# Turnings of chunks 4 and 5 as whole 128x128 blocks, every step in another fixed order, and the weights loaded behind the first inputs

## The chip, the cores and the metric

The kernel runs on one core of one Trainium2 chip. The metric is the device time of one execution in microseconds (us), and lower is better. The engines are named as in the profile: PE (TensorE) with its weight loads PEld, DVE (VectorE), ACT (ScalarE), POOL (GpSimd) and SP (SyncE, which here only issues transfers).

## The reference

A recurrent attention layer is followed by a feed-forward block with squared ReLU. There are 4 batches, 8 heads, 768 time steps and a head size of 40; the inputs r, k, v, w, a and b have the shape [4, 8, 768, 40] in float32.

```python
for t in range(S):                       # S = 768, per batch b and head h
    y[:, :, t] = einsum('bhd,bhde->bhe', rt, state)
    Sa = einsum('bhde,bhe->bhd', state, at)
    state = state * wt[:, :, None, :] - einsum('bhd,bhe->bhde', Sa, bt) \
            + einsum('bhd,bhe->bhde', vt, kt)
x = y.transpose(0, 2, 1, 3).reshape(B * S, H * D)     # 3072 x 320
h = maximum(x @ w_in, 0)                              # w_in  320 x 2048
out = (h * h) @ w_out                                 # w_out 2048 x 320
```

## The kernel before

The 768 time steps are cut into 12 chunks of 64. The state is carried from chunk to chunk; inside a chunk the recurrence is written as matrix products with a triangular mask. All matrix work is in bf16 with sums in float32.

For each chunk c there are these steps; a step's name is its kind and its chunk, and a helper issues it, so the profile gives it the helper's line.

- Loads `ldw`, `lda`, `ldk`, `ldb`, `ldv`, `ldr`: SP issues two transfers of 160 KB for each, into buffers that exist twice. A load waits until the chunk two before has been read out of its buffer.
- Preparation. `ln`, `hi` and `lo` take the logarithm of w and split it into two bf16 parts; `cf` and `ce` sum it along time on PE, and `ef`, `ef i` and `eg` take exponentials on ACT (L595, L598, L528). `castK`, `castB`, `castA`, `castR` and `castV` turn inputs into bf16. In chunks 0 to 7 the casts are then turned on PE (transposed by a matrix product with the identity): `TK` (k and b), `TA`, `TR`, and later `BK` (the scaled k and b back), `TV` (v), `TS` (the state) and `XT` (the output). Their results are copied or multiplied out of PSUM by `tK`, `tA`, `tR`, `bK`, `tV`, `tS` and `xt`.
- Recurrence: `EN` and its mask `mEN` (L752), `AS` (needs the state of the chunk before), `EV`, `u0`, `NU`, `u1`, then the new state `SC`, `S` and `s`.
- Output of the recurrence: `CX` and `mCX`, `RS`, `Y`, `y`, `yd`, `XT`, `xt`.
- Feed-forward block in four parts u0 to u3: `F` (inner dimension 256) and `FL` (the last 64), `f` (ReLU), `q` (square), `O` (with w_out), then `o` and the store `st`. Chunk 11 splits `O` into `OA`, `OB` and `OC`.

A turning exists in two forms. The first turns the 64 upper and the 64 lower rows apart (`tp`, L409), with two small products side by side in the array. The second turns a whole 128x128 block in one product (`tpw`, L412), so that it has half as many products. The set `WHOLE` says for which chunks the second form is used.

The weights are loaded by POOL, which also converts them to bf16: `lwi 0 k0 x0` to `k1 x3` (eight pieces of w_in, one for each half of the inner dimension and each part u), `lwl 0` (the last 64 rows of w_in, two transfers) and `lwo 0 x0` to `x7` (w_out). Being instructions of POOL's queue, they wait for whatever POOL does ahead of them.

The order of everything is written out by hand, or rather as a long string `ORDER`: for every step it names the engine and, on PE, the PSUM slot 0 to 3 (`PE2 TK 4`). `WD2` entries are two products of ones whose result nobody reads; they fill PE's time at the start. Each engine runs its own steps strictly in that order, and a step waits for its inputs by semaphores. So the string sets three things: which engine does a step that could run on two or three, what stands in front of it there, and which PSUM slot it waits for.

The two forms, in the steps TK, and the loop that issues the string (a few lines of each):

```python
        if c in WHOLE:                                            # L622, in turned_first
            ms = [tpw(lambda i=i, y=y: slot(hb, BF16)[:, y].rearrange(...)[:, :, i, :],
                      lambda i=i, y=y: tKB[y][:, i].rearrange("p q e -> p (q e)"))
                  for i in range(8) for y in range(2)]
        pe(f"TK {c}", *tmode(c), ms, reads=[("tKB", 0), ("tKB", 1)], writes=[hb], alloc=[hb])

        for entry in text.replace("\n", " ").split(";"):          # L64, Plan.issue
            where, name = entry.split(None, 1)
            ...
            for h in o.alloc:
                self.slot_of[h] = int(where[len(eng):])
```

Of the kernel before, what the change touches and what calls it, by code (L numbers as in the profile page):

```python
# [87 lines left out]
0; SP ldb 0; POOL zr 0; DVE lo 0; SP ldv 0; POOL castA 0; PE1 ce 0; POOL zv 2; PE2 cf 0; POOL zr
1; SP lda 1; PE3 WD2; ACT ef 0; PE0 TA 0; SP ldw 2; DVE castB 0; ACT ln 1; DVE castK 0; ACT ef 0
i; PE3 TK 0; POOL hi 1; DVE tA 0 g0; SP ldk 1; DVE zv 0; POOL lo 1; ACT eg 0; DVE tA 0 g1; PE2  # L90
WD2; DVE tK 0 g1; SP ldb 1; ACT castA 1; POOL castV 0 g1; POOL castV 0 g0; PE2 cf 1; DVE tK 0 g0;
SP ldr 0; PE0 TA 1; ACT ef 1 i; PE1 EN 0 g1; SP ldr 1; PE3 WD2; DVE mEN 0 g1; ACT ln 2; PE3 EN 0
g0; SP ldk 2; ACT ef 1; POOL castK 1; DVE mEN 0 g0; PE1 WD2; PE1 WD2; ACT castB 1; SP ldb 2; DVE
tA 1 g1; PE1 ce 1; PE2 EV 0; POOL hi 2; DVE zv 1; PE3 TK 1; ACT u0 0 w; DVE tA 1 g0; SP ldv 1;
POOL lo 2; ACT u0 0 s1; DVE u0 0 s0; DVE tK 1 g0; PE NU 0; PE0 WD2; ACT u1 0 x0s0; PE0 BK 0; SP
ldb 3; DVE tK 1 g1; ACT u1 0 x0s1; ACT u1 0 x1s0; DVE bK 0; SP ldw 3; ACT u1 0 x1s1; PE3 EN 1 g1;
DVE mEN 1 g1; ACT castR 1; PE0 EN 1 g0; PE2 S 0 g0; PE S 0 g1; ACT eg 1; DVE s 0; POOL castV 1 g0;
PE3 TV 0; ACT castV 1 g1; DVE mEN 1 g0; POOL zk 1; PE1 AS 1; POOL castR 0; ACT tV 0; DVE zk 2;
POOL castK 2; PE EV 1; SP ldr 2; PE2 TR 0; DVE u0 1 s0; PE0 TR 1; ACT tR 0 g0; DVE tR 0 g1; SP lda
3; ACT tR 1 g0; DVE tR 1 g1; PE3 CX 0 g0; PE2 TS 0; ACT ln 3; DVE castB 2; PE0 WD2; SP ldv 2; DVE  # L100
tS 0; ACT u0 1 s1; PE0 cf 2; ACT u0 1 w; DVE mCX 0 g0; PE2 CX 0 g1; ACT ef 2 i; PE NU 1; SP lda 2;
DVE mCX 0 g1; PE3 TK 2; ACT u1 1 x0s0; ACT ef 2; SP ldv 3; DVE u1 1 x0s1; PE2 Y 0; ACT u1 1 x1s0;
PE0 BK 1; DVE yd 0; DVE y 0; ACT u1 1 x1s1; DVE tK 2 g0; ACT bK 1; PE2 ce 2; PE1 TV 1; POOL hi 3;
SP ldk 3; DVE tK 2 g1; ACT castV 2 g1; POOL lo 3; PE0 SC 1; ACT eg 2; DVE tV 1; SP ldw 4; PE3 XT
0; POOL lwi 0 k0 x2; PE S 1 g0; ACT xt 0; PE S 1 g1; POOL castA 2; PE2 cf 3; DVE s 1; PE1 CX 1 g0;
POOL lwi 0 k1 x2; PE3 CX 1 g1; DVE mCX 1 g0; ACT ef 3; PE0 TA 2; ACT ef 3 i; DVE mCX 1 g1; PE1 BK
2; PE2 RS 1; DVE tA 2 g1; POOL castK 3; ACT castB 3; PE Y 1; DVE tA 2 g0; ACT castV 2 g0; POOL
castR 2; PE3 TS 1; DVE yd 1; ACT bK 2; POOL lwl 0; DVE y 1; PE0 EN 2 g0; DVE mEN 2 g0; PE2 XT 1;
POOL lwi 0 k0 x1; ACT xt 1; POOL lwi 0 k1 x1; DVE za 0; PE1 F 0 u2; ACT tS 1; POOL castA 3; PE0 F
1 u2; POOL lwi 0 k0 x0; POOL lwi 0 k1 x0; PE2 EN 2 g1; POOL lwo 0 x2; PE3 TK 3; DVE mEN 2 g1; POOL  # L110
lwi 0 k1 x3; POOL lwi 0 k0 x3; PE FL 0 u2; DVE tK 3 g0; PE FL 1 u2; ACT f 0 u2; POOL lwo 0 x1; PE2
FL 1 u1; POOL lwo 0 x0; DVE f 1 u2; PE F 1 u1; POOL lwo 0 x3; DVE tK 3 g1; PE1 FL 0 u1; ACT f 1
u1; PE F 0 u1; ACT q 0 u2; PE0 TR 2; POOL q 1 u1; PE3 F 0 u0; ACT tR 2 g0; ACT f 0 u1; PE2 F 1 u0;
ACT tR 2 g1; PE FL 0 u0; POOL q 0 u1; PE FL 1 u0; ACT f 0 u0; PE1 TA 3; DVE f 1 u0; PE0 AS 2; PE
EV 2; PE3 FL 1 u3; DVE u0 2 s0; ACT u0 2 s1; POOL lwo 0 x5; PE2 FL 0 u3; PE F 1 u3; ACT u0 2 w;
DVE tA 3 g1; POOL lwo 0 x4; PE F 0 u3; DVE tA 3 g0; POOL lwo 0 x7; ACT f 1 u3; DVE q 0 u0; POOL
lwo 0 x6; PE NU 2; DVE f 0 u3; PE1 EN 3 g0; ACT u1 2 x0s0; POOL q 1 u3; PE3 O 0 u0; ACT castV 3
g0; DVE mEN 3 g0; ACT u1 2 x0s1; PE O 0 u1; ACT castV 3 g1; DVE u1 2 x1s0; POOL za 1; PE2 BK 3;
ACT ln 4; DVE q 0 u3; PE O 0 u2; SP ldw 6; DVE u1 2 x1s1; ACT bK 3; PE1 EN 3 g1; SP ldk 4; PE0 ce
3; DVE mEN 3 g1; PE2 SC 2; ACT hi 4; PE S 2 g0; PE S 2 g1; ACT q 1 u0; PE O 0 u3; DVE s 2; POOL lo  # L120
4; SP ldb 4; ACT eg 3; PE1 AS 3; DVE o 0; PE EV 3; PE2 cf 4; SP ldw 5; DVE u0 3 s0; PE0 TV 2; ACT
ef 4 i; DVE q 1 u2; PE3 O 1 u0; ACT ef 4; DVE tV 2; ACT u0 3 s1; PE O 1 u1; DVE u0 3 w; SP lda 4;
ACT castB 4; PE2 CX 2 g1; ACT castK 4; PE0 CX 2 g0; DVE mCX 2 g1; PE NU 3; SP ldr 3; PE O 1 u2;
ACT u1 3 x0s0; DVE mCX 2 g0; ACT u1 3 x0s1; SP ldk 6; PE2 TK 4; ACT ln 5; PE O 1 u3; DVE tK 4 g0;
ACT u1 3 x1s0; SP ldr 4; POOL castA 4; ACT u1 3 x1s1; PE0 RS 2; DVE tK 4 g1; PE Y 2; ACT o 1; SP
ldv 4; PE1 TA 4; DVE yd 2; DVE y 2; PE3 ce 4; PE2 TV 3; POOL hi 5; DVE tA 4 g1; ACT castR 3; PE0
TS 2; DVE tA 4 g0; ACT eg 4; SP ldb 5; DVE tS 2; PE1 SC 3; ACT tV 3; PE S 3 g0; PE S 3 g1; PE3 XT
2; DVE s 3; PE0 TR 3; PE1 EN 4 g1; ACT xt 2; SP ldk 5; PE2 BK 4; DVE mEN 4 g1; POOL castV 4 g0;
ACT tR 3 g0; PE3 F 2 u0; ACT tR 3 g1; SP ldv 5; POOL lo 5; DVE bK 4; ACT castR 4; PE1 EN 4 g0; PE0
FL 2 u1; DVE mEN 4 g0; PE FL 2 u0; PE2 CX 3 g0; POOL castV 4 g1; ACT f 2 u0; PE F 2 u1; DVE mCX 3  # L130
g0; PE1 TS 3; POOL q 2 u0; ACT f 2 u1; SP st 0; PE3 AS 4; PE EV 4; DVE tS 3; ACT q 2 u1; PE2 CX 3
g1; PE0 TR 4; DVE mCX 3 g1; PE1 FL 2 u3; SP lda 5; POOL zg 0; PE F 2 u3; POOL castK 5; ACT tR 4
g0; ACT u0 4 w; POOL castB 5; DVE tR 4 g1; PE2 F 2 u2; SP ldv 6; ACT f 2 u3; DVE u0 4 s0; POOL
castV 5 g0; PE FL 2 u2; DVE u0 4 s1; PE0 TK 5; ACT f 2 u2; DVE q 2 u3; PE1 cf 5; PE NU 4; POOL q 2
u2; ACT ef 5 i; SP ldb 6; PE2 O 2 u0; DVE u1 4 x0s0; DVE tK 5 g1; ACT u1 4 x0s1; PE O 2 u1; SP ldw
7; POOL castA 5; ACT ef 5; DVE tK 5 g0; PE O 2 u2; ACT u1 4 x1s0; ACT u1 4 x1s1; PE1 RS 3; ACT ln
6; PE0 TA 5; PE Y 3; SP ldb 7; DVE tA 5 g0; PE3 ce 5; DVE y 3; PE O 2 u3; SP ldw 8; DVE yd 3; ACT
castB 6; DVE tA 5 g1; PE1 XT 3; ACT eg 5; PE0 TV 4; DVE xt 3; ACT hi 6; DVE tV 4; PE3 SC 4; PE S 4
g0; ACT o 2; PE S 4 g1; POOL lo 6; PE1 F 3 u0; DVE s 4; SP ldr 6; PE2 BK 5; POOL castK 6; PE FL 3
u0; DVE bK 5; PE0 CX 4 g0; ACT f 3 u0; PE3 cf 6; SP ldb 8; DVE mCX 4 g0; PE2 FL 3 u3; ACT ef 6; PE  # L140
F 3 u3; POOL q 3 u0; ACT ef 6 i; PE1 EN 5 g1; PE0 F 3 u2; DVE mEN 5 g1; SP st 1; ACT f 3 u3; POOL
castV 5 g1; PE3 EN 5 g0; PE FL 3 u2; DVE mEN 5 g0; PE1 CX 4 g1; POOL q 3 u3; ACT f 3 u2; PE2 FL 3
u1; SP ldv 7; PE F 3 u1; DVE mCX 4 g1; ACT ln 7; PE3 AS 5; ACT f 3 u1; PE EV 5; POOL castV 6 g0;
PE0 ce 6; DVE u0 5 w; PE1 O 3 u0; ACT u0 5 s1; DVE u0 5 s0; SP ldk 7; ACT eg 6; DVE q 3 u2; PE2 RS
4; DVE q 3 u1; PE NU 5; SP ldr 5; PE Y 4; DVE hi 7; ACT u1 5 x0s0; PE0 TK 6; DVE yd 4; ACT u1 5
x0s1; POOL lo 7; DVE y 4; SP lda 6; PE O 3 u1; ACT u1 5 x1s0; DVE tK 6 g1; ACT u1 5 x1s1; SP lda
7; PE O 3 u2; ACT ln 8; DVE tK 6 g0; PE O 3 u3; DVE hi 8; SP ldw 10; PE2 XT 4; PE3 TV 5; DVE xt 4;
ACT castR 5; PE0 TS 4; DVE tV 5; ACT o 3; PE2 TR 5; POOL castA 6; ACT tR 5 g1; PE1 FL 4 u3; PE F 4
u3; ACT tR 5 g0; DVE lo 8; SP lda 8; DVE tS 4; PE3 SC 5; ACT f 4 u3; PE S 5 g0; PE S 5 g1; PE2 CX
5 g1; DVE s 5; PE0 cf 7; POOL q 4 u3; PE1 FL 4 u1; DVE mCX 5 g1; ACT ef 7 i; PE3 CX 5 g0; SP ldw  # L150
9; PE F 4 u1; ACT ef 7; DVE zg 1; DVE mCX 5 g0; PE2 F 4 u0; POOL castB 7; ACT f 4 u1; PE0 TA 6;
PE3 ci 8 h0; DVE tA 6 g1; PE FL 4 u0; ACT castK 7; POOL q 4 u1; PE1 RS 5; DVE tA 6 g0; ACT ei 8
h0; PE Y 5; SP ldb 9; ACT f 4 u0; PE0 TS 5; DVE yd 5; PE3 TK 7; DVE y 5; POOL castA 7; ACT tS 5;
PE2 ci 8 h1; SP st 3; DVE tK 7 g1; PE1 F 4 u2; POOL q 4 u0; ACT ei 8 h1; DVE tK 7 g0; PE FL 4 u2;
PE0 XT 5; ACT f 4 u2; SP ldk 8; POOL castV 6 g1; PE2 BK 6; DVE xt 5; PE3 EN 6 g0; POOL q 4 u2; ACT
bK 6; PE1 EN 6 g1; DVE mEN 6 g0; PE0 FL 5 u3; PE F 5 u3; SP st 2; ACT ln 9; DVE mEN 6 g1; PE2 ce
8; PE3 FL 5 u1; PE F 5 u1; ACT eg 8; DVE f 5 u3; POOL hi 9; PE1 TA 7; POOL castR 6; ACT f 5 u1;
# [947 lines left out]
```

## Time and profile before

| | |
|---|---|
| runs | 236.65, 237.68, 237.89 us, median 237.68 |
| profiled execution | 238.23 us, of which the span of the trace is 236.2 us |
| granted TensorE clock | 0.997 |
| busy: PE, DVE, ACT, POOL | 217.5, 179.0, 165.2, 117.3 us |
| read from and written to HBM | 28.84 MB, 3.93 MB |

All times in the text are microseconds from the start of the span. A row of the timeline begins with its start and its length, then engine, line, operation, output and inputs; in brackets stands how long the engine was idle before it and what ended that. A busy PE is not PE at its peak, because products are pipelined and their ends are modelled.

### The profile page before, as it was taken

The numbers are of one execution on the slowest core, as the hardware profiler recorded it, in microseconds if no ns is written. First come the engines' busy times: TensorE is split into PE (matmuls) and PEld (weight loads), VectorE is DVE, ScalarE is ACT, GpSimd is POOL, SyncE is SP. The second block draws the span as 40 slices with busy tenths as digits, with TensorE's granted clock in tenths as the row PEclk, the third lists the DMA queues.
The fourth block names the chain that finished last, engine by engine and source line by source line (L and its number), as shares of the span: only waits on it lengthen the run. The fifth ranks groups of instructions, "written<-read, shape, count | busy, mean of one in ns | idle before, by whom it ended". The sixth has DMA issues, their size and how long they took to land.

```text
span 236.2 us, 12291 instructions
## 1 busy us (share of the span) xinstructions
PE 217.5 (92%) x5632; PEld 165.1 (70%) x5632; DVE 179.0 (76%) x234; ACT 165.2 (70%) x227; POOL 117.3 (50%) x120
## 2 busy tenths in 40 slices
...
GB/s 126 205 221 227 160 167 184 153 151 126 113 196 214 184 174 180 171 158 221 115 140 153 141 121 134 119 162 121 117 82 153 164 117 92 123 173 57 2 3 110
DMA packets 104575, 33.84 MB, mean 143 GB/s; under 512 B 88652, under 2 KB 104524, under 8 KB 104524
## 3 DMA queue, kind: packets, MB, share of 16 engines
...
q8 instruction: 44, 0.72, 1.3%
...
HBM read 28.84 MB, written 3.93 MB: 139 GB/s over the span
## 4 chain that ended last, share of the span: by engine, by line
PE 75%; DVE 11%; DMA 4%; ACT 3%; POOL 3%; issue 2%; SPq 1%; ACTq 0%; POOLq 0%
PE pb L405 65%; PE pb L409 6%; DMA raw_w<-in_w_dram 4%; PE pb L412 3%; DVE KBT L631 2%; DVE CX L752 2%; DVE EN L752 2%; DVE Yb L901 1%; DVE AT L667 1%; DVE KBT L635 1%; ACT NZ L391 1%; POOL lo L399 1%; ACT lnW L497 1%; POOL VU L395 1%; ACT VU L391 1%
## 5 line engine op out<-in xcount | busy, mean ns | idle before, releaser
L976 POOL TENSOR_TENSOR G<-G 128x1024 bf16<-128x1024 bf16 x20 | 38.2, 1916 | 43.4 <-ACT G L968 39.1
L405 PE MATMUL pb<-WOUT,G 128*128 128x320 bf16 (+1 forms) x400 | 57.4, 294 | 0.2 <-issue 0.2
L405 PE MATMUL pb<-XT,WIN 128*128 128x256 bf16 x384 | 48.7, 273 | 0.3 <-DVE KBT L631 0.2
L968 ACT ACTIVATE G<-pb 128x1024 bf16<-128x1024 f32 x36 | 36.8, 1024 | 15.9 <-PE pb L405 15.7
L405 PEld LDWEIGHTS <-G 128*128 128x128 bf16 x400 | 36.1, 98 | 14.4 <-issue 1.4
L405 PEld LDWEIGHTS <-WIN 128*128 128x128 bf16 x384 | 34.7, 98 | 9.0 <-issue 3.8
L752 DVE TENSOR_TENSOR EN<-pb,MSK 128x1024 bf16<-128x1024 f32 x24 | 28.9, 1220 | 9.4 <-PE pb L405 9.2
L752 DVE TENSOR_TENSOR CX<-pb,MSK 128x1024 bf16<-128x1024 f32 x24 | 28.8, 1219 | 5.5 <-PE pb L405 5.4
L399 POOL TENSOR_TENSOR KB<-raw_kb,iG 128x640 bf16<-128x640 f32 x8 | 14.8, 1863 | 15.8 <-ACT iG L688 15.8
L391 ACT ACTIVATE VU<-pb 64x320 bf16<-64x320 f32 x40 | 17.2, 431 | 4.6 <-PE pb L405 3.9
L970 DVE TENSOR_SCALAR G<-pb 128x1024 bf16<-128x1024 f32 x12 | 14.6, 1220 | 4.6 <-PE pb L405 4.4
L405 PE MATMUL pb<-XT,WLAST 64*128 64x256 bf16 x192 | 16.5, 271 | 0.0
L399 POOL TENSOR_TENSOR lo<-lnW,hi 128x640 bf16<-128x640 f32 x7 | 9.9, 1419 | 11.4 <-ACT hi L391 4.1
L901 DVE TENSOR_TENSOR Yb<-pb,Gex 128x128 bf16<-128x128 f32 (+1 forms) x24 | 12.2, 551 | 4.0 <-PE pb L405 3.9
L497 ACT ACTIVATE lnW<-raw_w 128x640 f32<-128x640 f32 x12 | 11.4, 946 | 5.4 <-DMA raw_w<-in_w_dram 4.4
L978 ACT ACTIVATE G<-G 128x1024 bf16<-128x1024 bf16 x13 | 13.5, 1054 | 1.0 <-DVE G L970 0.9
L395 POOL CAST VU<-raw_v 64x640 bf16<-64x640 f32 x14 | 10.0, 716 | 7.0 <-DMA raw_v<-in_v_dram 6.6
L391 ACT ACTIVATE osb<-pb 128x640 f32<-128x640 f32 (+2 forms) x10 | 6.4, 637 | 9.8 <-PE pb L405 9.8
L391 ACT ACTIVATE NZ<-pb 64x320 bf16<-64x320 f32 (+1 forms) x20 | 8.7, 433 | 6.2 <-DVE NZ L388 3.9
L667 DVE TENSOR_TENSOR AT<-pb,GT 128x512 bf16<-128x512 bf16 x16 | 10.5, 676 | 1.9 <-PE pb L409 1.8
L391 ACT ACTIVATE RT<-pb 128x512 bf16<-128x512 bf16 x17 | 9.4, 596 | 3.2 <-PE pb L409 3.2
L974 DVE TENSOR_TENSOR G<-G 128x1024 bf16<-128x1024 bf16 x15 | 11.4, 766 | 0.3
...
## 6 DMA issues: line engine op xcount, KB each, us to landing
...
```

The lines of the kernel that those rows point to most:

```text
L391: alts.append(("ACT", c_act(n), lambda: nc.scalar.activation(out=o_(), in_=i_(), func=ACTF.Copy, scale=1.0 if scale is None else scale)))
L399: return [("POOL", 40 + 2.35 * n, lambda: nc.gpsimd.tensor_tensor(out=o_(), in0=a_(), in1=b_(), op=op)), ("DVE", c_dve(n), lambda: nc.vect ...
L405: return lambda: nc.tensor.matmul(out=o_(), lhsT=l_(), rhs=r_(), start=start, stop=stop, skip_group_check=True)
L409: return lambda: nc.tensor.transpose(out=o_(), in_=i_(), identity=IDb[rows(g), :])
L497: ew(f"ln {c}", [("ACT", c_act(640), lambda: nc.scalar.activation(out=lw[:] if early else lw[:].rearrange("p (s f m) -> p s m f", s=2, m=4 ...
L667: ew(f"tA {c} g{g}", [("DVE", c_dve(512), lambda g=g: nc.vector.tensor_tensor(out=AT[q2][:, NP * g:NP * g + NP].rearrange("p m (k i) -> p ...
L752: ew(f"m{nm} {c} g{s}", [("DVE", c_dve(1024), lambda: nc.vector.tensor_tensor(out=dst[q2][:, s].rearrange("p q i t -> p (q i) t"), in0=slo ...
L901: return [("DVE", c_dve(2 * (f1 - f0)), lambda: nc.vector.tensor_tensor(out=Yb[q2][:, :, to:to + f1 - f0], in0=slot(hy, FP32)[:, :, f0:f1] ...
L968: ("ACT", c_act(1024), lambda gb=gb, hf=hf: nc.scalar.activation(out=gb, in_=slot(hf, FP32)[:], func=ACTF.Relu)),
L970: ("DVE", c_dve(1024), lambda gb=gb, hf=hf: nc.vector.tensor_scalar(out=gb, in0=slot(hf, FP32)[:], scalar1=0.0, scalar2=None, op0=ALU.max))],
L976: ("POOL", 1900, lambda gv=gv: nc.gpsimd.tensor_tensor(out=gv, in0=gv, in1=gv, op=ALU.mult)),
L978: ("ACT", c_act(1024), lambda gv=gv: nc.scalar.activation(out=gv, in_=gv, func=ACTF.Square))],
```

## The change

Two constants of the program change. `WHOLE` is extended by chunks 4 and 5:

```diff
-    WHOLE = range(4)
+    WHOLE = range(6)
```

In these two chunks TK, BK and TV have 16 products of 128x128 in place of 32 of 64x128, TA, TR and TS have 8 in place of 16, and XT has 6 in place of 12. The program has 156 products fewer.

The string `ORDER` is another one, with the same 1050 entries apart from the engines and slots. Its first lines before and after:

```diff
-ORDER = """SP ldw 0; PE0 WD2; SP lda 0; POOL zs 0; DVE zs 1; SP ldk 0; POOL zk 0; SP ldw 1; ACT ln 0; POOL hi
+ORDER = """SP ldw 0; PE0 WD2; SP ldk 0; PE1 WD2; SP ldb 0; SP ldw 1; ACT ln 0; SP lda 0; DVE hi 0; DVE lo 0;
...
```

Two places of it matter below. A row with a number behind it (x2) stands for so many equal rows in a line. The first is POOL's queue where the weights are loaded. The names are buffers: `tKB` (k, b), `tAr` (a), `tR` (r) and `VU` (v) are cast from the inputs `raw_...`, `WIN` and `WLAST` are w_in, `G` is the squaring step q. Before, from the log parts of chunk 3 on:

```order
L395 CAST hi_86<-lnW_85 128x16x40
L399 TENSOR_TENSOR lo_87<-lnW_85,hi_86 128x16x40
L1044 DMA WIN_141<-in_moe_w_in_dram 128x512
L395 CAST tAr_95<-raw_a_79 128x2x8x40
L1044 DMA WIN_141<-in_moe_w_in_dram 128x512
L395 CAST tKB_93<-raw_kb_78 128x2x8x40
L395 CAST tR_114<-raw_r_81 128x2x8x40
L1039 DMA WLAST_142<-in_moe_w_in_dram 64x4x256 x2
```

Now, from castB of chunk 2 to the second group of weights:

```order
L395 CAST tKB_94<-raw_kb_77 128x2x8x40
L395 CAST tAr_95<-raw_a_79 128x2x8x40
L354 MEMSET KB_108 128x32x24
L354 MEMSET VU_111 128x32x24
L354 MEMSET tA_113 128x16x24
L1044 DMA WIN_141<-in_moe_w_in_dram 128x512
L1039 DMA WLAST_142<-in_moe_w_in_dram 64x4x256 x2
L1044 DMA WIN_141<-in_moe_w_in_dram 128x512 x3
L395 CAST tAr_96<-raw_a_80 128x2x8x40
L395 CAST VU_111<-raw_v_83 64x2x8x40 x2
L395 CAST hi_86<-lnW_85 128x16x40
L395 CAST tKB_93<-raw_kb_78 128x2x8x40
```

Six pieces of the weights have moved ahead of the casts of chunk 3's k (`raw_kb_78`), where before one piece stood ahead of the cast of chunk 2's a and a second one ahead of chunk 3's k.

The second place is SP's queue, from the 15th to the 24th load of the program. Before:

```order
L430 DMA raw_v1_84<-in_v_dram 64x16x40 x2
L435 DMA raw_kb1_78<-in_b_dram 128x1x320 x2
L424 DMA raw_w1_76<-in_w_dram 64x16x40 x2
L465 DMA raw_r0_81<-in_r_dram 128x1x320 x2
L435 DMA raw_a1_80<-in_a_dram 128x1x320 x2
L430 DMA raw_v0_83<-in_v_dram 64x16x40 x2
L435 DMA raw_a0_79<-in_a_dram 128x1x320 x2
L430 DMA raw_v1_84<-in_v_dram 64x16x40 x2
L435 DMA raw_kb1_78<-in_k_dram 128x1x320 x2
L424 DMA raw_w0_75<-in_w_dram 64x16x40 x4
```

Now:

```order
L435 DMA raw_a0_79<-in_a_dram 128x1x320 x2
L435 DMA raw_kb0_77<-in_b_dram 128x1x320 x2
L435 DMA raw_kb0_77<-in_k_dram 128x1x320 x2
L430 DMA raw_v0_83<-in_v_dram 64x16x40 x2
L435 DMA raw_a1_80<-in_a_dram 128x1x320 x2
L430 DMA raw_v1_84<-in_v_dram 64x16x40 x2
L435 DMA raw_kb0_77<-in_k_dram 128x1x320 x2
L435 DMA raw_kb1_78<-in_k_dram 128x1x320 x2
L435 DMA raw_kb1_78<-in_b_dram 128x1x320 x2
L424 DMA raw_w0_75<-in_w_dram 64x16x40 x2
```

The last row of before holds two loads, w of chunk 4 and of chunk 6. Chunk 3's b, the 16th load before, is now the 23rd; its k is the 22nd in place of the 23rd, and one input of chunk 4 (`raw_kb0_77<-in_k_dram`) stands ahead of both. Chunk 3's w, the 17th load before, is the 14th now, and chunk 2's k and b, the 13th and 14th before, are the 17th and 16th.

More of the change, by code (lines that the diff above doesn't have):

```diff
@@ L86 @@
 O_AFTER = 0
-ORDER = """SP ldw 0; PE0 WD2; SP lda 0; POOL zs 0; DVE zs 1; SP ldk 0; POOL zk 0; SP ldw 1; ACT ln 0; POOL hi
[L88 to L157, printed above, removed]
```

184 lines of the change are left out of this document (127 added, 57 removed).

## The prediction

> **What bounds the kernel now.** I read the page first, for the span and the busy shares:
>
> ```profile
> span 236.2 us, 12291 instructions
> PE 217.5 (92%) x5632; PEld 165.1 (70%) x5632; DVE 179.0 (76%) x234; ACT 165.2 (70%) x227; POOL 117.3 (50%) x120
> PE 75%; DVE 11%; DMA 4%; ACT 3%; POOL 3%; issue 2%; SPq 1%; ACTq 0%; POOLq 0%
> ```
>
> PE is busy for 92% of the span and carries 75% of the chain of work that ended last. Where the other 8% lie is told by the windows. Their columns are the window, its length, then the busy time of PE, PEld, DVE, ACT and POOL, the granted clock, the share of the 16 DMA engines and GB/s.
>
> ```profile
> 0.00:20.00 20.00, 12.00 (x161) 7.40 (x165) 11.75 (x24) 9.10 (x11) 9.92 (x24) 1.00 0.96 186
> 20.00:40.00 20.00, 16.25 (x508) 13.39 (x500) 17.73 (x25) 15.17 (x24) 7.90 (x10) 1.00 0.86 180
> 40.00:60.00 20.00, 18.96 (x442) 15.16 (x439) 15.85 (x20) 14.80 (x20) 18.29 (x25) 1.00 1.05 150
> 120.00:140.00 20.00, 19.42 (x613) 14.86 (x613) 14.90 (x19) 16.96 (x24) 17.91 (x14) 1.00 0.74 143
> ...
> 60.00:220.00 160.00, 157.78 (x4423) 119.40 (x4421) 129.51 (x164) 120.31 (x167) 75.50 (x61) 1.00 0.69 143
> ```
>
> PE idles 8.0, 3.75 and 1.0 us in the first three windows, while the DMA engines are busy for 0.86 to 1.05 of the time. From 60 to 220 us it idles 2.2 us in 160, at most 0.6 in a window of 20. So there are two regimes: up to about 55 us the inputs and weights come in and the steps wait for one another, and behind that PE has work at every moment. Whatever makes PE's work longer adds to the time in full, and whatever PE loses before 55 us is not caught up, because the work behind it fills the rest.
>
> **The turnings of chunks 4 and 5.** The chain in order of time (start, length, engine and line, number of products) has both forms side by side, L412 for whole blocks and L409 for halves:
>
> ```profile
> 55.27 0.55 PE pb L412 x8
> 61.83 0.89 PE pb L412 x16
> 67.82 1.00 PE pb L412 x16
> 80.46 0.47 PE pb L409 x32
> 83.90 0.45 PE pb L412 x8
> 85.41 0.23 PE pb L409 x16
> 95.66 0.34 PE pb L412 x6
> 96.00 0.57 PE pb L409 x32
> 118.68 0.34 PE pb L409 x16
> 175.02 0.19 PE pb L409 x12
> ```
>
> Each step comes with two lengths that differ by 0.10 or 0.11 (0.89 and 1.00, 0.47 and 0.57, 0.23 and 0.34). In the program's order the longer one stands where the next step uses another shape of the array. So a change of shape costs 0.10 us, and like is to be compared with like. A step of 16 whole blocks costs 0.42 us more than 32 halves, and there are three of them in a chunk (TK, BK, TV). One of 8 costs 0.21 more than 16 halves (0.55 less 0.34), again three (TA, TR, TS), and XT costs 0.15 more (0.34 less 0.19). That is 1.26 + 0.63 + 0.15 = 2.04 us for a chunk and 4.1 us for two. F and O use the whole array too, and so a whole turning next to them changes no shape. Counting along PE's order, neighbours of different shape fall from 216 to 195, which gives back 21 x 0.10 = 2.1 us. Net: **+2.0 us** on PE, where nothing hides it. The bounds are 0, if more of the changes of shape are hidden, and 4.1, if the new neighbours don't save any.
>
> The copies out of PSUM don't get cheaper: the multiplication by the decay has the same length in both forms.
>
> ```profile
> L631 DVE TENSOR_TENSOR KBT<-pb,iGT 128x1024 bf16<-128x1024 bf16 x8 | 9.5, 1216 | 0.5 <-PE pb L412 0.5
> L635 DVE TENSOR_TENSOR KBT<-pb,iGT 128x1024 bf16<-128x1024 bf16 x8 | 9.4, 1217 | 0.2 <-ACT iGT L598 0.2
> ```
>
> **The start, up to chunk 2's state step (AS 2).** Here the order decides. Three rows of the timeline mark the path of before: chunk 0's TK waits for k and b, chunk 3's `ln` (in front of chunk 1's u0 on ACT) waits for its w, the 17th load, and AS 2 begins at 55.76.
>
> ```profile
> 12.24 1.89 PE L412 MATMUL pb<-IDQ,tKB 128*128 128x128 bf16 x16 [1.06 <-DVE tKB L386]
> 31.82 0.74 ACT L497 ACTIVATE lnW<-raw_w 128x640 f32<-128x640 f32 x1 [0.97 <-DMA raw_w<-in_w_dram]
> 55.76 0.43 PE L405 MATMUL pb<-STb,AT 64*64 64x40 bf16 x32
> ```
>
> What gets earlier: k and b of chunk 0 are now the 2nd and 3rd load in place of the 3rd and 5th, so TK 0 can follow `cf` and `ce` at about 10.1, some 2.1 us sooner. Little of this lasts, since tA 0 now stands behind both tK 0 and a `lo` on DVE, and chunk 1's tA and tK follow two casts there. Chunk 3's w is the 14th load, so the wait at 31.82 goes. Late next is then not DVE, but what POOL and ACT wait for, the loads of chunk 3.
>
> These are the 22nd and 23rd load. The 23rd of before was chunk 3's k, and POOL waited for it until 42.07:
>
> ```profile
> 39.55 0.75 POOL L1044 DMA_DIRECT2D WIN<-in_moe_w_in_dram  x1
> 42.07 0.72 POOL L395 CAST tKB<-raw_kb 128x640 bf16<-128x640 f32 x1 [0.57 <-DMA raw_kb<-in_k_dram]
> 44.63 1.09 POOL L1044 DMA_DIRECT2D WIN<-in_moe_w_in_dram  x2
> 45.68 1.55 PE L405 MATMUL pb<-XT,WIN 128*128 128x256 bf16 x11
> ```
>
> The first weights went out at 39.55, when the inputs were nearly in. Now six pieces go out behind castB 2, castA 2 and three memsets. The cast needs the 16th and 17th load, which I put at 31.5 by the row of 31.82; with two casts of 0.72 and memsets of 0.74, 0.74 and 0.4 the pieces start at about 34.5. The transfers' own view shows what that means. Its rows are a queue's packets, megabytes and share of the 16 engines: q1 has SP's loads, q0 the weights. The first row is of the window 30 to 39, the next two of 40 to 46, the last of 46 to 56.
>
> ```profile
> q1 hardware_dynamic: 4968, 1.63, 89.5%
> ...
> q0 software_dynamic: 510, 0.37, 53.0%
> q1 hardware_dynamic: 2358, 0.63, 49.3%
> ...
> q0 software_dynamic: 2195, 1.55, 115.2%
> ```
>
> Alone, the loads had 89.5% of the engines and the weights 115.2% (packets of several queues overlap). Together they had about half each. So the six pieces are paid for by the loads behind them: 6 x 0.131 MB = 0.79 MB at the 0.155 MB/us of the last row are 5.1 us. Chunk 3's b lands at 42.07 + 5.1 = 47.2. Then castK 3 (0.72) and the issue of two more pieces (1.09) follow in POOL's queue, and those land 4.5 us after their issue:
>
> ```profile
> WIN<-in_moe_w_in_dram POOLq DMA_DIRECT2D x8, 128.0 KB, 4.5
> L405 PE MATMUL pb<-XT,WIN 128*128 128x256 bf16 x384 | 48.7, 273 | 0.3 <-DVE KBT L631 0.2
> L405 PE MATMUL pb<-XT,WLAST 64*128 64x256 bf16 x192 | 16.5, 271 | 0.0
> ```
>
> They are the part u1 of w_in, so F 0 u1 starts at 47.9 + 0.8 + 4.5 = 53.2. Queued behind it on PE are F 1 u0, FL 1 u3, FL 1 u0, EN 3 g1, F 1 u3 and AS 2. With 48.7/48 = 1.01 us for an F, 16.5/48 = 0.34 for an FL and 0.3 for EN, AS 2 starts at 53.2 + 3 x 1.01 + 2 x 0.34 + 0.3 = 57.2, that is 1.4 later than before. By then PE has also done less. Ahead of AS 2 stood three F, three FL and a TR that are now behind it; in their place are two F, two FL, `ce` and EN of chunk 3. The difference is 1.01 + 0.34 + 0.5 - 0.4 - 0.3, about 1.1 us. Together the start costs **+2.5 us**. Both ends: without the sharing F 0 u1 is reached by its other inputs (y and yd of chunk 1 on DVE) at about 51, AS 2 at 55.0, and the start costs +0.3; if chunk 0's lead of 2.1 us lasted as well, -1.0. If the loads behind chunk 3's b slow the next pieces too, it is 2 us more.
>
> **Behind AS 2** PE idled 2.2 us in all from 60 to 220 (the last window above). The new order has other neighbours there. I take **-0.5 us**, with bounds of -2.2 and +2. The end, three partial products of chunk 11 and their stores, changes by 0.1 to 0.2 at most, since only the last evacuation grows:
>
> ```profile
> 231.50 0.44 ACT L391 ACTIVATE osb<-pb 128x320 f32<-128x320 f32 x1 [5.45 <-PE pb L405]
> 232.60 0.30 ACT L391 ACTIVATE osb<-pb 128x160 f32<-128x160 f32 x1 [0.67 <-PE pb L405]
> ```
>
> The sum is 2.0 + 2.5 - 0.5 = +4.0 us against the profiled execution of 238.23 (its span is 236.2). That execution lies 0.55 above the median of 237.68, so I put the same difference on the median: **241.6 us**.
>
> **The rivals.** (A) *The start keeps its lead.* Chunk 0's TK is 2.1 us sooner and no step waits for the weights, because the inputs of chunk 3 have landed by then; the start costs -1.0, the idle time behind it is used up (-2.2), the turnings +2.0. That is -1.2 us, 236.5; with the turnings at their lower bound of 0 it is 234.5, and I put it at 235.8. For it speaks that DMA is at only 0.86 of its engines from 20 to 40; against it the halved share of q1. It decides at castK 3: if POOL gets to it before 45 us, F 0 u1 waits for nothing. (B) *The weights are hidden anyway*, the start +0.3, the turnings +2.0, the idle time -2.2: +0.1, 237.8. (C) *The weights come later still.* If the two pieces of u1 land 4 us later, because w and r behind them share the engines too, PE stands still for longer than it ever did behind 10 us, and it could get slower by it. These rows of products of ones, at the start and later, show it at half speed:
>
> ```profile
> 1.13 1.03 PE L1068 MATMUL pb<-ones 128*128 128x512 bf16 x2 [1.13 <-DVE ones L257]
> 16.99 0.60 PE L1068 MATMUL pb<-ones 128*128 128x512 bf16 x2
> ```
>
> The price is 3.4 us of waiting plus 1 to 2 us of slow products: 246. The Trainium skill has a rule for this (TensorE: Matmul & The Clock Gate, section on the HAM clock gate): the array falls to half its clock after some 3.4 us without work and needs about as long to come back. The profile's granted clock is 1.00 in that first window, so it doesn't show the half speed that the two rows show. By the rule alone my forecast would have nothing added, since none of its waits is as long as that.
>
> **How the numbers follow.** Forecast 0.52, A 0.22, B 0.13, C 0.13. The low end of the range takes in A and the better bound of the shapes, the high end the worse bounds of start and turnings together, short of C's full price: 235.5 to 245.5. About 0.5% is what a measurement here can tell from no change, so 236.5 and 238.9 are the limits: faster 0.22 (A), same 0.13 (B), slower 0.65 (the forecast and C).
>
> **What would show it.** Right: L412 rows of 0.9 to 1.0 and 0.45 to 0.55 in chunks 4 and 5; q1's share at about half between 35 and 45; a wait of POOL or ACT for chunk 3's k or b until 46 to 48; an idle PE or a long F around 53, and AS 2 at 56.5 to 58. Wrong: POOL's castK 3 at 44 or sooner with AS 2 before 55 (then A or B), or PE's busy time not longer although the turnings are whole.

## The result

The changed kernel takes 244.73 us (median; 244.44 to 245.40) where the kernel before takes 237.30 on the same chip: 1.029 times as long (95% interval 1.023 to 1.034). By that ratio it is slower by 6.8 us (the medians lie 7.4 apart); the prediction had 3.9 us. A second measurement on another chip (below, beside the experiments) gave 1.024 (1.020 to 1.028). The profiled execution of the changed kernel took 244.44 us with a span of 242.5, which is 6.3 above the span of before; the profiled execution of before (238.23) lay 0.9 above its median.

The page of the changed kernel: PE is busy 3 us longer and still carries most of the chain that ended last, but SP's queue now has 11% of it (1% before).

```profile
span 242.5 us, 11995 instructions
PE 220.5 (91%) x5476; PEld 169.4 (70%) x5476; DVE 179.6 (74%) x235; ACT 161.3 (66%) x224; POOL 123.6 (51%) x122
PE 70%; SPq 11%; DVE 5%; DMA 5%; POOL 3%; issue 3%; ACT 2%; POOLq 0%
```

The windows, with the columns as before. PE is busy for 15.73 and 17.48 us in the second and third (16.25 and 18.96 before), although some of its work ran at half speed: the granted clock is 0.83 from 10 to 30 us.

```profile
0.00:20.00 20.00, 12.12 (x186) 7.09 (x186) 11.69 (x25) 10.85 (x14) 6.28 (x18) 0.91 0.90 185
20.00:40.00 20.00, 15.73 (x420) 12.99 (x420) 17.55 (x22) 11.06 (x21) 13.51 (x23) 0.91 0.93 174
40.00:60.00 20.00, 17.48 (x431) 13.96 (x432) 18.14 (x24) 13.66 (x15) 11.47 (x16) 1.00 0.98 173
...
60.00:220.00 160.00, 156.51 (x4188) 121.07 (x4187) 124.26 (x155) 113.63 (x163) 92.31 (x68) 1.00 0.69 138
...
10.00:20.00 10.00, 7.64 (x137) 4.77 (x135) 7.43 (x9) 7.50 (x11) 3.44 (x5) 0.83 0.93 198
20.00:30.00 10.00, 7.31 (x172) 6.09 (x173) 9.49 (x13) 4.99 (x10) 4.33 (x7) 0.83 0.95 210
```

The chain in order of time shows the turnings of chunks 4 and 5 in their new form (L412: TK 4, TR 4, TK 5), and the old form from chunk 6 on (L409):

```profile
75.65 0.89 PE pb L412 x16
88.15 0.45 PE pb L412 x8
91.99 1.00 PE pb L412 x16
110.11 0.47 PE pb L409 x32
```

The timeline rows of the start that answer to those of before: TK 0 (12.24 before), chunk 3's `ln` (31.82), POOL's cast of chunk 3's k (42.07) and AS 2 (55.76). In the middle stands NU 0, a step of chunk 0's recurrence that turns out to matter; it began at 21.94 before.

```profile
9.24 1.89 PE L412 MATMUL pb<-IDQ,tKB 128*128 128x128 bf16 x16
...
23.88 0.62 PE L405 MATMUL pb<-NZ,EN 64*64 64x40 bf16 x32
...
35.45 0.74 ACT L497 ACTIVATE lnW<-raw_w 128x640 f32<-128x640 f32 x1
...
47.61 0.72 POOL L395 CAST tKB<-raw_kb 128x640 bf16<-128x640 f32 x1 [7.31 <-DMA raw_kb<-in_b_dram]
...
58.38 0.43 PE L405 MATMUL pb<-STb,AT 64*64 64x40 bf16 x32
```

The view of the transfers from 35 to 46 us, and what SP's own queue waited for from 20 to 45 us (total, times, longest): weights (q0) and loads (q1) have about half of the engines each, and SP stood still for 5.4 us.

```profile
q0 software_dynamic: 1120, 0.79, 60.3%
q1 hardware_dynamic: 2245, 1.19, 46.6%
...
SPq L435 <- ACT VU L391: 5.4, 1, 5.4
```

SP's wait is the load of chunk 4's k. It stands ahead of chunk 3's k and b in SP's queue, and its buffer comes free only when ACT has done castK 2, at 36.8. (The view names VU, the step behind castK 2 on ACT; this is castK 2's row.)

```profile
36.07 0.74 ACT L391 ACTIVATE tKB<-raw_kb 128x640 bf16<-128x640 f32 x1
```

To compare all runs I split each span into four parts. PE's own work is the sum of its steps at the price of their rows in the trace of before (from one start to the next where nothing waits: F 0.88, O 1.09, a turning of 16 whole blocks 0.90, of 32 halves 0.47, a change of shape 0.095). The waits up to AS 2 are AS 2's start less the work ahead of it; then follow the waits behind AS 2, and the tail behind PE's last step. Fills count as work, and what half clock adds counts as waiting.

| kernel | PE's work | waits to AS 2 | waits behind | tail | span |
|---|---|---|---|---|---|
| before | 207.4 | 18.7 | 6.5 | 3.7 | 236.2 |
| changed | 209.7 | 22.7 | 6.3 | 3.8 | 242.5 |
| changed, second chip | 209.7 | 21.9 | 5.6 | 3.8 | 241.0 |

So the 6.3 us are 2.3 of work, 4.0 of waits at the start, -0.2 behind it and 0.2 at the end.

### The profile page after: what moved, and what is told of

Read it like the earlier page. It is cut to its first block, busy times and chain, and to the rows that moved or that the text cites. A ratio compares the mean times of both kernels' runs of the same rounds, so it can differ in the third digit from the quotient of the medians.

```text
span 242.5 us, 11995 instructions
## 1 busy us (share of the span) xinstructions
PE 220.5 (91%) x5476; PEld 169.4 (70%) x5476; DVE 179.6 (74%) x235; ACT 161.3 (66%) x224; POOL 123.6 (51%) x122
## 2 busy tenths in 40 slices
DMA packets 104574, 33.82 MB, mean 139 GB/s; under 512 B 88652, under 2 KB 104524, under 8 KB 104524
## 4 chain that ended last, share of the span: by engine, by line
PE 70%; SPq 11%; DVE 5%; DMA 5%; POOL 3%; issue 3%; ACT 2%; POOLq 0%
PE pb L405 59%; PE pb L412 8%; SPq L435 5%; PE pb L409 3%; DMA raw_v<-in_v_dram 3%; SPq L430 2%; POOL KB L399 2%; SPq L452 1%; DMA raw_kb<-in_k_dram 1%; SPq L424 1%; POOL VU L395 1%; DVE STb L825 1%; DVE KBT L631 1%; DVE CX L752 1%; DVE RT L386 1%
## 5 line engine op out<-in xcount | busy, mean ns | idle before, releaser
L976 POOL TENSOR_TENSOR G<-G 128x1024 bf16<-128x1024 bf16 x25 | 47.0, 1891 | 26.4 <-ACT G L968 26.3
L968 ACT ACTIVATE G<-pb 128x1024 bf16<-128x1024 f32 x41 | 41.6, 1022 | 14.3 <-PE pb L405 13.8
L391 ACT ACTIVATE VU<-pb 64x320 bf16<-64x320 f32 x37 | 15.9, 431 | 10.2 <-PE pb L405 8.4
L395 POOL CAST VU<-raw_v 64x640 bf16<-64x640 f32 x16 | 11.4, 714 | 15.5 <-DMA raw_v<-in_v_dram 15.0
L391 ACT ACTIVATE NZ<-pb 64x320 bf16<-64x320 f32 (+1 forms) x25 | 10.8, 432 | 10.5 <-DVE NZ L388 7.3
L631 DVE TENSOR_TENSOR KBT<-pb,iGT 128x1024 bf16<-128x1024 bf16 x12 | 14.2, 1209 | 3.3 <-ACT hi L391 2.2
L395 POOL CAST tKB<-raw_kb 128x640 bf16<-128x640 f32 x8 | 5.9, 757 | 16.8 <-DMA raw_kb<-in_b_dram 12.0
L595 ACT ACTIVATE GT<-pb 128x1024 f32<-128x1024 f32 x8 | 8.2, 1021 | 7.2 <-PE pb L405 6.4
L405 PEld LDWEIGHTS <-EN 64*64 64x64 bf16 x768 | 8.8, 110 | 5.4 <-issue 5.1
L391 ACT ACTIVATE osb<-pb 128x640 f32<-128x640 f32 (+2 forms) x12 | 7.8, 649 | 7.2 <-PE pb L405 7.1
L391 ACT ACTIVATE RT<-pb 128x512 bf16<-128x512 bf16 x14 | 8.1, 594 | 5.5 <-PE pb L412 3.5
```

The costliest lines, as they stand in the source:

```text
L391: alts.append(("ACT", c_act(n), lambda: nc.scalar.activation(out=o_(), in_=i_(), func=ACTF.Copy, scale=1.0 if scale is None else scale)))
L395: lambda: nc.gpsimd.tensor_copy(out=o_(), in_=i_())))
L405: return lambda: nc.tensor.matmul(out=o_(), lhsT=l_(), rhs=r_(), start=start, stop=stop, skip_group_check=True)
L631: ew(f"tK {c} g{g}", [("DVE", c_dve(1024), lambda g=g, gm=gm: nc.vector.tensor_tensor(out=KBT[q2][:, :, g].rearrange("p m (k i) -> p m k i ...
L968: ("ACT", c_act(1024), lambda gb=gb, hf=hf: nc.scalar.activation(out=gb, in_=slot(hf, FP32)[:], func=ACTF.Relu)),
L976: ("POOL", 1900, lambda gv=gv: nc.gpsimd.tensor_tensor(out=gv, in0=gv, in1=gv, op=ALU.mult)),
```

## The experiments

Theories: (T1) the prediction's, whole turnings make PE's work longer, and weights ahead of the inputs delay chunk 3's loads and by them AS 2. (T2) SP's blocked queue delays those loads. (T3) the start is lost earlier, in VectorE's queue. (T4) it is lost by PE's half clock. Each run is compared with runs of before on the same chip; "ratio" is to those.

**Turnings back to halves in the changed order.**

```diff
-    WHOLE = range(6)
+    WHOLE = range(4)
```

> The changed kernel with chunks 4 and 5 turned by halves again, its order kept. Turnings priced by rows (the prediction's step, counted over this order with its changes of array shape): PE's work is 3.0 us shorter, so 244.7 - 3.0 = 241.8 us, and PE's busy time falls by 2.5 to 3.5 us while AS 2 stays at 58 to 58.5 us. Rival, the turnings are hidden or free: 244 to 245 us, AS 2 as before.

Measured: 246.36 us, ratio 1.038 (1.033 to 1.043): not faster than the changed kernel, rather slower. In its profiled execution (244.28, the shortest of the six) PE's work is 206.7, 3.0 us less as priced, the waits to AS 2 are 22.6 as they were, but the waits behind it rose from 6.3 to 9.2. PE's busy time doesn't fall (220.7; 220.5 in the changed kernel), where 2.5 to 3.5 us were expected. The timeline shows the largest: TK 5 stands still for 1.78 us ahead of its last product, with no releaser ("issue").

```profile
91.67 0.64 PE L409 MATMUL pb<-IDb,tKB 64*128 64x64 bf16 x31
94.08 0.19 PE L409 MATMUL pb<-IDb,tKB 64*128 64x64 bf16 x1 [1.78 <-issue]
```

Neither theory said that: the work is saved and comes back as waits, 1.7 of the 2.9 us as pauses like this one (3.5 us behind AS 2, 1.8 in the changed kernel).

**Whole turnings in the order of before.**

```diff
-    WHOLE = range(4)
+    WHOLE = range(6)
```

> The kernel before with chunks 4 and 5 turned as whole blocks, its order kept. Turnings priced by rows: 4.1 us for 14 steps, and with this order's changes of shape (216 to 220) 4.7 us, so 237.3 + 4.5 = 241.8 us (241.3 to 242.2). Rival, the turnings are hidden or free: 237 to 238 us. If they cost even in the order that was written for them, the change's order gives back half of it.

Measured: 242.51 us, ratio 1.020 (1.014 to 1.025), that is +4.6 us by the ratio (the medians lie 5.9 apart). Split: work 212.0, waits to AS 2 18.0, behind 7.7, tail 3.7. Here the price of the turnings is paid in full, as the prediction's rows had it.

**No whole turnings at all, order of before.**

```diff
-    WHOLE = range(4)
+    WHOLE = ()
```

> The kernel before with all eight chunks turned by halves, its order kept. By the row prices PE's work is 8.7 us shorter (198.6 against 207.4), some of it in the waits of the start, where it brings nothing: by the prices alone 230 to 233 us. Theory of the pauses at every 128th product (halves use up products faster than new ones come in): the work saved comes back as pauses of PE without a releaser, 92 or 93 beyond multiples of 128, and the time is 234.5 to 238.

Measured: 244.28 us, ratio 1.027 (1.022 to 1.033), slower than any of the forecasts. PE's work is 8.7 us shorter, the waits to AS 2 are 27.2 in place of 18.7, those behind 13.3 in place of 6.5. PE's waits from 12 us on, first two rows of before, then two of this kernel; "issue" has grown from 1.6 to 8.5 us:

```profile
PE pb L405 <- issue: 1.3, 6, 0.3
PE pb L409 <- issue: 0.3, 1, 0.3
...
PE pb L405 <- issue: 5.8, 8, 1.3
PE pb L409 <- issue: 2.7, 6, 0.6
```

Counted through the trace, the pauses stand ahead of products that are 92 to 95 beyond a multiple of 128: in this kernel behind the 479th, 863rd, 991st, 1757th, 1885th, 2397th, 2525th, 2781st, 3164th and five later ones, in the run with four whole chunks in the changed order behind the 1885th, 3037th, 3549th and three others, in before behind the 2653rd, 2780th, 3292nd and others. 128 products are 256 instructions of PE, since each has its weight load. The queue of instructions on the pages has 44 packets where there are 5632 products and 43 where there are 5476:

```profile
q8 instruction: 44, 0.72, 1.3%
...
q8 instruction: 43, 0.70, 1.2%
```

That is a packet of 16 KB for each 128 products. The times of the packets fit as well. In 13 traces 54 pauses of 0.07 us and more stand 91 to 95 products beyond a multiple of 128, and each of them ends 1.2 to 1.8 us behind the end of the packet with that multiple's number. (The pause of 1.78 us above stands at the 14th multiple; the 14th packet moved from 91.6 to 92.5 us, and PE went on at 94.08.) So the pauses end with the arrival of packets. That a late packet is their cause rests on these times alone, since no run changed the packets. Halves use up 32 products in 0.47 us, whole blocks 16 in 0.90: nearly four times as many in a microsecond. What is shown is the balance: in the changed order halves save 3.0 us of work and waits grow by 2.9; here they save 8.7 and waits grow by 15.3, 6.9 of it by these pauses. Most of the rest is half clock: the granted clock is 0.74 from 20 to 40 us and 0.91 from 40 to 60, 1.00 in both in before, which makes 7.0 us of clock. PE's busy time falls by 1.0 us only (216.5; 217.5).

**Chunk 4's k behind chunk 3's loads.** In SP's queue of the changed kernel:

```diff
-SP ldk 4; ... SP ldk 3; ... SP ldb 3;
+SP ldk 3; ... SP ldb 3; SP ldk 4;
```

> The changed kernel with the load of chunk 4's k moved from in front of chunk 3's k and b to right behind them in SP's queue; nothing else. Theory of the blocked queue (SP stood still from 31.8 to 36.8 us because chunk 4's k waits until ACT has read chunk 2's k): chunk 3's k and b are issued 4 to 5 us sooner and land at 43 to 44 us instead of 47.5, castK 3 begins at 44 us, AS 2 at 55.5 to 56.5 instead of 58.4, and the time is 242 to 243 us. Theory of the shared DMA engines (the prediction's): they were full anyway with six pieces of weights, b of chunk 3 lands at 46.5 or later and the time is 244 to 245 us. Theory that the time was lost before 32 us (slow cast of chunk 1's k and half clock): POOL and DVE still come late, AS 2 at 57.5 or later, 243.8 to 244.7.

Measured: 242.57 us, ratio 1.025 (1.021 to 1.030), the changed kernel's on the second chip. The rows (this file's lines are 6 higher) say why:

```profile
43.02 0.72 POOL L401 CAST tKB<-raw_kb 128x640 bf16<-128x640 f32 x1 [3.71 <-DMA raw_kb<-in_b_dram]
...
58.28 0.43 PE L411 MATMUL pb<-STb,AT 64*64 64x40 bf16 x32
```

Chunk 3's k and b are there 4.6 us sooner, and AS 2 doesn't move. (The time lies where T2 had it, at 242 to 243, but that was forecast from the first chip's 244.7, and the ratio is the changed kernel's.) The changed kernel's own trace agrees: TK 3, which needs chunk 3's k, begins at 52.70 without a wait, 4.4 us behind its cast. T2 falls, and with it the last part of T1: in the changed order chunk 3's loads aren't what AS 2 waits for. The 11% that the chain of the page gave to SP's queue was no time that could be had back.

**Early weights in the order of before.** In POOL's queue:

```diff
-castK 2; ... hi 3; lo 3; lwi 0 k0 x2; castA 2; lwi 0 k1 x2; castK 3; ... lwl 0; lwi 0 k0 x1; lwi 0 k1 x1;
+castK 2; lwi 0 k0 x2; lwi 0 k1 x2; lwl 0; lwi 0 k0 x1; lwi 0 k1 x1; ... hi 3; lo 3; castA 2; castK 3; ...
```

> The kernel before with six transfers of the weights (four pieces of w_in and the two of its last rows) moved ahead in POOL's queue to right behind castK 2, as early as in the changed kernel; its order is otherwise kept, and so SP's loads are not blocked by chunk 4's k. Theory of the shared DMA engines: 0.79 MB at 0.155 MB/us are 5.1 us, chunk 3's k lands at 45 to 47 us instead of 42.0, AS 2 starts at 57 to 59 instead of 55.8, and the time is 238.5 to 240.5 us. Theory of the blocked queue: the loads keep most of the engines, AS 2 within 0.5 of 55.8, 237 to 237.8 us. Early weights could also help, since u1 of w_in lands sooner: AS 2 at 53 to 55, 235 to 236.5 us.

Measured: 240.80 us, ratio 1.018 (1.014 to 1.023).

```profile
45.63 0.72 POOL L401 CAST tKB<-raw_kb 128x640 bf16<-128x640 f32 x1 [1.79 <-DMA raw_kb<-in_k_dram]
...
43.09 0.21 PE L411 MATMUL pb<-UTI,hi 64*128 64x64 bf16 x2 [1.80 <-ACT Gex L534]
...
52.02 1.07 PE L418 MATMUL pb<-IDQ,tKB 128*128 128x128 bf16 x16
...
59.74 0.43 PE L411 MATMUL pb<-STb,AT 64*64 64x40 bf16 x32
```

Chunk 3's k comes 3.6 us later (5.1 expected), AS 2 4.0 later; the waits behind it fall by 1.8. But AS 2 doesn't hang on chunk 3's k here either: TK 3 (the row of 52.02) begins without a wait, 5.7 us behind the end of its cast. PE's long wait is ahead of `cf 3` (43.09; 39.88 in before), for `eg 2` on ACT. That stands behind the cast of chunk 2's v, which ACT could begin only at 41.58, after 2.75 us of waiting for the load; in before it began at 38.29 without a wait. A pause of 0.84 us and a stretch at half clock from 43.8 to 47.2 come on top. So the mechanism that the prediction named is real in the order of before: weights ahead of the inputs delay a load on which AS 2 hangs. It is another load than the prediction had.

**The changed kernel again, and two steps off VectorE.** The next four runs share a chip.

> The changed kernel once more, on the same chip as the three runs beside it, so that they can be compared directly. 244 to 245.5 us, AS 2 at 58.2 to 58.5 us. Theory that PE's pauses without a releaser belong to a count of products (they stand at the 2397th, 3293rd and 3421st product in the first profile, which are 18, 25 and 26 times 128 plus 93): they stand at the same products again. Rival, chance: elsewhere.

Measured: 242.66 us, ratio 1.024 (1.020 to 1.028); AS 2 at 57.52. Of the pauses, the one behind the 3421st product is there again, those behind the 2397th and 3293rd are not, and a new one stands behind the 3677th: the distance of 128 holds. The pause behind the 3421st is in all seven traces of this order with chunks 4 and 5 whole (0.5 to 1.4 us), also in the one with eight more products ahead of it, so it goes by the count of products and not by the step; the others come and go.

```diff
-DVE lo 1; ... DVE castK 1; ACT eg 1;
+POOL lo 1; ... ACT eg 1; ACT castK 1;
```

> The changed kernel with two steps taken off VectorE: lo 1 on POOL (idle there from 8.6 to 16.4 us) and castK 1 on ACT behind eg 1. Theory that the start is lost in VectorE's queue: cf 1 no longer waits 1.4 us for lo 1, TK 1 begins at about 20 us instead of 21.55, the waits of PE up to 30 us fall by 1.5 to 2.5 us, AS 2 begins at 56.3 to 57.2 instead of 58.4, and the time is 1.2 to 2.2 us below the changed kernel's. Theory of the prediction (chunk 3's loads behind the weights set AS 2): AS 2 within 0.3 of 58.4 and the time unchanged.

Measured: 241.57 us, ratio 1.018 (1.014 to 1.023), 1.1 us below the run beside it; the intervals overlap, so the traces have to carry it. NU 0 and AS 2, first of the changed kernel on this chip, then of this one:

```profile
23.02 0.62 PE L405 MATMUL pb<-NZ,EN 64*64 64x40 bf16 x32
57.52 0.43 PE L405 MATMUL pb<-STb,AT 64*64 64x40 bf16 x32
...
18.71 1.04 PE L412 MATMUL pb<-IDQ,tAr 128*128 128x128 bf16 x8 [1.47 <-POOL tAr L395]
...
22.11 0.44 PE L405 MATMUL pb<-NZ,EN 64*64 64x40 bf16 x32
56.61 0.44 PE L405 MATMUL pb<-STb,AT 64*64 64x40 bf16 x32
```

Both are 0.9 us sooner, and NU 0 is back at its time of before (21.94). One pair of traces is little. But NU 0 begins at 23.02 to 23.88 in the four traces of the changed order in which nothing ahead of it was moved, and at 22.11 to 22.90 in the three with these two steps moved (this run and two below). So T3 holds for this part; it is 0.9 and not 1.5 to 2 because castA 1 on POOL is late next (the row of 18.71), behind castV 0, which waits for its load.

**More fill against the half clock.**

```diff
-PE3 WD2; ... PE3 cf 1; ... PE3 TK 1;
+PE3 WD5; ... PE3 cf 1; ... PE3 WD5; PE3 TK 1;
```

> The changed kernel with five products of ones in place of two ahead of cf 1 and five new ones ahead of TK 1, where PE stood idle for 1.4 and 2.0 us; nothing else is moved. Theory of the clock: the two stretches of half speed from 15.0 to 18.4 and from 21.8 to 25.2 us go away, TK 1 takes 1.1 us instead of 2.2, AS 2 begins 0.7 to 1.5 us sooner, and the time is 0.7 to 1.5 us below the changed kernel's. Theory that VectorE's queue sets the start whatever PE's clock: AS 2 within 0.4 of 58.4 and the same time. Theory of the count of products: the pauses stay at 93 beyond a multiple of 128, that is eight products earlier in the steps than in the changed kernel.

Measured: 242.68 us, ratio 1.024 (1.019 to 1.029), the same as beside it. The mean granted clock was 0.999 or 1.000 in five of the six runs, against 0.976 to 0.984 in all runs of the changed kernel on this chip: the half speed is gone and the time is not. The five have a median of 242.12, 0.5 us less than the run beside it and within the spread of both, where the theory of the clock had 0.7 to 1.5. The two traces of the changed kernel say the same: the one on this chip has 10.2 us at half clock (granted 0.74 and 0.75 in the windows of 10 to 20 and 20 to 30 us), the first one 6.8, and the one with more of it has the sooner AS 2, by 0.9. T4 falls as a cause that can be measured. (The profiled run was the one at 0.984, and AS 2 came later in it, 59.41, since EV 0 waited 1.5 us for a cast of v.) The Trainium skill (TensorE: Matmul & The Clock Gate, section Part 1: The HAM clock gate) states that the gate watches a free-running window of about 3.4 us. The first trace's rows of 10 to 30 us agree: 0.83 over 10 us is 3.4 us at half clock, once in each.

**VectorE relieved further, and chunk 4's k later.** As above, with `DVE lo 3` turned into `POOL lo 3` and `SP ldk 4` behind `SP ldb 3`.

> The changed kernel with lo 1 and lo 3 on POOL, castK 1 on ACT (all three off VectorE), and the load of chunk 4's k behind chunk 3's k and b. VectorE's queue as the cause: the gains of the start (1.2 to 2.2 us) and of lo 3 (up to 0.8 us, since VectorE works without a pause from 39 to 50 us) add up, AS 2 begins at 55.5 to 56.5 us, with the later load the time is 2.5 to 4 us below the changed kernel's, 240.5 to 242. The prediction's cause (weights and loads share the DMA engines): AS 2 not before 57.8, 243 to 244.5.

Measured: 241.73 us, ratio 1.017 (1.011 to 1.022). Split: waits to AS 2 21.9, behind 3.2.

```profile
22.90 0.62 PE L405 MATMUL pb<-NZ,EN 64*64 64x40 bf16 x32
57.55 0.43 PE L405 MATMUL pb<-STb,AT 64*64 64x40 bf16 x32
```

A miss: the gains didn't add up. NU 0 begins at 22.90 and not at 22.11 as with the two steps alone: chunk 0's v landed later, and TA 1, whose cast stands behind that of v, waited 2.1 us in place of 1.5. With lo 3 gone from VectorE the stretch from NU 0 to AS 2 is 34.65, about as in every run of this order before (34.35 to 34.82), whether chunk 3's k was cast at 43.0 or 47.6. In before it is 33.82, with about 0.6 us more of PE's work in it.

**Chunk 1's recurrence sooner.** On top of lo 1 and castK 1 off VectorE (`u0 1` moves along on ACT and VectorE, and one fill is dropped):

```diff
-PE1 TS 0; PE2 ce 2; PE3 TV 0; PE1 AS 1; PE EV 1; ... PE2 CX 0 g1; PE3 BK 1; PE NU 1;
+PE1 AS 1; PE2 TS 0; PE EV 1; PE3 ce 2; PE2 TV 0; ... PE NU 1; PE3 CX 0 g1; PE2 BK 1;
```

> The run with lo 1 and castK 1 off VectorE, and in addition chunk 1's recurrence (AS 1, EV 1, u0 1, NU 1) moved ahead of TS 0, ce 2, TV 0 and CX 0 on PE and ahead of tV 0 on VectorE; one fill of two products dropped. In five runs of the changed order AS 2 began 34.3 to 34.7 us after NU 0, whatever the loads, the clock and lo 3 did. Theory that this stretch is a chain set by the order of the recurrence's steps: it shrinks to 32.7 to 33.8 us, AS 2 at 55 to 56.2 us, and the time is 0.7 to 1.8 us less than in the run with the two steps moved, 1.009 to 1.015 of before. Rival, a resource holds it (VectorE's total work, or the loads of chunk 2): the stretch stays within 0.4 of 34.5 and the time at 1.016 to 1.021.

Measured: 244.25 us, ratio 1.030 (1.024 to 1.035): wrong by both theories. NU 1 does begin 1.9 us sooner (31.34), but AS 2 comes at 60.39:

```profile
47.49 1.89 PE L405 MATMUL pb<-XT,WIN 128*128 128x256 bf16 x8 [1.99 <-DMA WIN<-in_moe_w_in_dram]
...
60.39 0.43 PE L405 MATMUL pb<-STb,AT 64*64 64x40 bf16 x32
```

F 0 u3 waits 2.0 us for the sixth of the early pieces, which was issued at 38.15 and landed at 47.44 (43.8 in the changed kernel). It then ran at half speed (1.89 us; 1.04 in the changed kernel), with a granted clock of 0.66 from 47 to 52 us. A wait of 1.4 us for the copy tR 1, behind lo 3 on VectorE, comes on top. In the changed kernel F 0 u3 had 2.1 us to spare behind that piece (43.8 to 45.9); with the recurrence sooner the early weights are late next.

**Halves of the two orders.** First the order of before up to EV 2 and the changed one for the rest, then the reverse:

```diff
-ORDER = changed
+ORDER = before[: EV 2] + [steps of changed not yet issued]
```

> The order of before up to and with EV 2, behind it the changed kernel's order for all steps that are left (one PSUM slot chosen anew); chunks 4 and 5 as whole blocks. PE's work by the row prices: 210.3 us against 207.4 of before and 209.7 of the changed kernel. Theory that the start's order costs 3 to 4 us and whole turnings with their new neighbours 2 to 3: AS 2 at 55 to 56 us, 3 to 4.5 us below the changed kernel, 238.8 to 240.2 us where before has 237. Theory that the rest of the order (or the turnings alone) holds the loss: 241 to 243.5.

> The changed kernel's order up to and with EV 2, behind it the order of before for all steps that are left (one slot anew); chunks 4 and 5 by halves. PE's work by the row prices: 206.9 us. Theory that the start's order costs 3 to 4 us by itself: AS 2 at 57.3 to 58.5 us, 239.5 to 241 us where before has 237. Theory that the loss lies behind it: 236.5 to 238.

Measured: 245.17 us, ratio 1.035 (1.029 to 1.041), and 251.67 us, ratio 1.065 (1.060 to 1.070). Inconclusive on what they were made for. In the second the waits behind AS 2 are 16.1 us, 10 of them from 60 to 80 us, at the seam; PE waits for ACT there, and once 2.3 us without a releaser:

```profile
PE pb L405 <- ACT NZ L391: 4.1, 2, 3.5
```

(The trace of the first isn't read: its execution took 249.11 us, more than any other of its runs.) Each order fits only its own continuation, so the parts can't be priced by cutting it. No version that was run beats the kernel before.

## Why the prediction came out as it did

The side and the signs of its terms were right, and the time lies within its range, near the upper end. The size was not right: +4.0 against 6.3 in the profiled execution (4.8 in that of the second chip, against the same trace of before).

- *The turnings, +2.0.* The work is 2.3 us longer, L412 rows of 0.89, 1.00 and 0.45 as priced, and the order of before pays the full price (+4.6 by the run, 4.1 by the rows without changes of shape). One reading of the rows was wrong without harm: the longer lengths stand where the step ahead uses another shape, not the step behind. TV 2 (1.00) follows `cf 4` and precedes O, BK 3 (0.89) stands between two O. The count of neighbours is the same either way. What the step left out is the number of instructions. It held "on PE, where nothing hides it"; in the changed order halves would have cost the same again in waits, most of them pauses. So the turnings belong to the change, but undoing them there gains nothing.
- *The start, +2.5.* It cost 4.0 (3.2 on the second chip). The times along the path came out near: chunk 3's cast at 47.6 (47.2), the two pieces of u1 landed at 52.8 (53.2), F 0 u1 at 54.6 (53.2), AS 2 at 58.4 (57.2). That is luck, since the path was the wrong one: F 0 u1 began 1.8 us behind its weights and waited for nothing, and the sign "an idle PE or a long F around 53" didn't come. The step that failed is "Late next is then not DVE, but what POOL and ACT wait for, the loads of chunk 3." NU 0 was 1.9 us late at 23.9, ten us before the first weights went out, and with the loads 4.6 us sooner AS 2 stayed. VectorE was late next, as the sentence ahead of it had begun to say: its `lo` of chunk 1 behind tK 0 made cf 1 wait 1.4 us, and its casts of chunk 1, which ran beside POOL's `lo`, made TK 1 wait 2.0. (The rows below are PE's waits up to 60 us: total, times, longest. The last one is of before up to 56 us, where it is TK 0's wait.) The sharing of the DMA engines was read rightly from the view of the transfers, and early weights delay AS 2 by 4.0 us in the order of before, by way of chunk 2's v; the price was put on a kernel in which PE didn't wait for the loads of chunk 3. That SP's queue would stand still for 5.4 us was missed too, and cost nothing.

```profile
PE pb L412 <- DVE tKB L386: 2.1, 2, 2.0
PE pb L405 <- DVE lo L401: 2.1, 2, 1.4
...
PE pb L412 <- DVE tKB L386: 1.1, 1, 1.1
```

- *Behind AS 2, -0.5, and the end, 0.2.* Measured -0.2 (-0.9) and 0.2.
- *The rivals.* A was to be decided by castK 3 before 45 us. It came at 47.6; but at 43.0, with chunk 4's k behind it, A didn't come true either, so the sign was a wrong one. B's premise came true, for no step of PE in the changed kernel waited for weights, but the start cost 4.0 and not 0.3 on another path. C's half speed came (clock 0.83 from 10 to 30 us), at another place than C had it, and without a measurable price; only the run with chunk 1's recurrence sooner had it where C did, behind a wait for weights.
- *Open.* Of the 3 to 4 us of waits at the start, the runs account for about 0.9 by the two steps on VectorE. By the prices of the rows, about 2.8 us of the first trace's are lost ahead of NU 0: it begins 1.9 us late, with 0.8 us less work ahead of it, most of that a fill. The other 1.3 lie between NU 0 and AS 2, a stretch that takes 0.7 us longer for 0.6 us less work; VectorE ends 3.5 us of PE's waits there, 2.1 in before. It isn't chunk 3's loads, lo 3 or the clock; which steps' order makes it, the runs don't say. No run put the weights late in the changed order, so that their early place costs nothing there is read from the traces alone.
